# Attention and gated convolution on one core: a wider pitch for V, one product per second part, and a key copy on another engine

## The chip, the core and the metric

The kernel runs on one core of a Trainium2 chip. The core has five engines that follow programs of their own and meet at semaphores: TensorE (PE, matmuls, with its weight loads shown apart as PEld), VectorE (DVE), ScalarE (ACT), GpSimd (POOL), and SyncE (SP), which here only issues DMAs. Each engine works through its instructions in the order in which the program issued them. The metric is the device time of one execution in microseconds (us), lower is better. Before the change it is 219.84 us, the median of three runs that range from 218.36 to 220.60 us.

## The reference, cut to what matters

There are 8 batches with 8 heads each, 576 positions and a head size of 64. The mask works in blocks of 64 positions: a query sees all keys of its own block and of the blocks before it.

```python
scores = scale * np.matmul(q, k.transpose(0, 1, 3, 2))
scores = np.where(block_i >= block_j, scores, -1e9)
attn = softmax(scores)                       # over the keys
x = np.matmul(attn, v)                       # then heads side by side: 512 columns
gate_pre[s] = sum over k of conv_w[k] * x[s - 4 + k]      # causal convolution, 5 taps
out = (sigmoid(gate_pre) * (x @ w_val)) @ w_out
```

## The kernel before, in words

Two heads make a pair; there are 32 pairs, four to a batch, and the main loop (L536) takes two of them, a and z = a + 1, in each of 16 turns. Everything is unrolled, and the order on every engine is the order in which the lines run: the program is written under a manual schedule, with no planner that moves instructions. Tiles are guarded region by region: an instruction waits for the last writer of the elements that it reads.

For one pair the work is this.

- **Loads and casts.** SP loads K, Q and V as 32-bit floats (`load_qk`, L99, and `load_v`, L112). `cast_qk` (L126) and `cast_v` (L130) turn them into 16-bit floats, on POOL but for the first casts. V goes into the tile `ve` as rows of 64 elements, each followed by a one (the ones are written once, at L463), so that a product with V also gives the sum of the exponentials. The last 64 keys of V are loaded by batch and stand in `vtail`.
- **Transposes.** `trans` (L137) has PE transpose K or Q into PSUM, and DVE copies the result into `kT` or `qT` (L151). `kT` holds nine key blocks of 64. For K a second copy (L154) puts key blocks 6 and 8 once more into slots 9 and 11, with zeros standing in slot 10.
- **Scores and exponentials.** `scores` makes three chunks of a pair, 0, 1 and 2, of 512 columns for each head. Only chunk 1 reads slots 9 to 11. The chunks alternate between two PSUM buffers (`S`). `exps` has ACT take the exponential of a chunk into `pt` (L189). After chunk 1 POOL copies a part into `pd` (L192) and clears a masked part (L196); after chunk 2 it clears another (L199). `burst` (L201) issues the scores of two chunks and then their exponentials.
- **Product with V.** `pv` (L205) has two parts. Part 0 makes query blocks 0 and 1 (six matmuls), part 1 query blocks 2 and 3 and the last 64 queries (24 matmuls). Each matmul has 128 columns of `pt` as weights and one row group of `ve` (65 columns) as the moving operand. DVE takes reciprocals of the sums (L231) and multiplies them in: four groups of 64 columns on 128 partitions (L233), and in part 1 two more groups on 64 partitions (L237). The result is `xn`, whose fifth column block belongs to the last 64 queries; its lower 64 partitions are cleared once at the start (L450).
- **Gated unit.** `xt_pair` transposes `xn` (PE, then DVE at L248), of whose columns only the first 576 are used. `gate` makes the convolution with diagonal weights on PE, a DVE step (L262) and a tanh on ACT (L265). `val` (PE, then DVE at L277) and `out_tile` (PE, then ACT at L292, then a store) are kept in a list, and `filler` spreads them between the other steps. All matmul outputs other than scores share four PSUM buffers.

Ahead of the loop POOL gets, in this order, the cast of Q of pair 1, of V of pair 0, of the batch's V tails, of K and Q of pair 2 and of V of pair 1 (L525 to L530); only then come the four calls of `trans` for pairs 0 and 1 (L531 to L534). In the loop each `trans` of K stands just behind a cast of V:

```python
burst([(a, 0), (a, 1)])          # L546
...
burst([(a, 2), (z, 0)])          # L561
...                              # POOL: casts of K and Q of pair z + 2
cast_v(a + 2)                    # L572
trans(a + 2, "k")                # L573
pv(a, 0)
...
burst([(z, 1), (z, 2)])          # L594
cast_v(z + 2)                    # L596
trans(z + 2, "k")                # L597
pv(a, 1)
```

The weights `w_val` and `w_out` are loaded by DMAs that POOL issues in the first turn (L584). A slow exact path behind a flag is not taken with this data.

Of the kernel before, what the change touches and what calls it, by code (L numbers as in the profile page):

```python
# [16 lines left out]
def kernel(  # L17
# [10 lines left out]
    nc = tc.nc  # L28
    fp32 = mybir.dt.float32
    fp16 = mybir.dt.float16  # L30
    AF = mybir.ActivationFunctionType
    ALU = mybir.AluOpType
# [9 lines left out]
    def mm(out, lhsT, rhs, start=True, stop=True):  # L42
        nc.tensor.matmul(out=out, lhsT=lhsT, rhs=rhs, start=start, stop=stop,  # L43
                         skip_group_check=True)
# [3 lines left out]
    def const(shape, dtype, name):  # L48
        return cpool.tile(shape, dtype, tag=name, name=name)
# [10 lines left out]
    NV = 6  # L60
    NPT = 4
    NX = 4
    ves = [const([128, 2, 4, 65], fp16, f"ve{i}") for i in range(NV)]

    pts = [const([128, 2 * 1536 + 64], fp16, f"pt{i}") for i in range(NPT)]
    NT = 6
# [7 lines left out]
    xns = [const([128, 5, 128], fp16, f"xn{i}") for i in range(NX)]  # L74
# [15 lines left out]
    def bank(name, dtype=fp32):  # L90
        return psM.tile([128, 512] if dtype == fp32 else [128, 1024], dtype,
                        tag="misc", name=name)
# [44 lines left out]
    def trans(p, name):  # L137
        src = c16.pop((name, p))
        ps = bank("ps_tr", fp16)
        for t in range(6):  # L140
            nc.tensor.transpose(out=ps[:, 96 * t:96 * t + 96], in_=src[:, t, :, :],  # L141
                                identity=ident16[0:96, 0:96])
        if name == "k":
            dst = kTs[p % NT][:, 0:9, :].rearrange("p n x -> p (n x)")
        else:
            dst = qTs[p % NT][:, :]
        src = ps[:, 0:SEQ]
        if p < WIDE:
            dst = dst.rearrange("p (s t) -> p s t", t=6)
            src = src.rearrange("p (t s) -> p s t", t=6)  # L150
        nc.vector.tensor_copy(out=dst, in_=src)  # L151
        if name == "k":
            K = kTs[p % NT]
            nc.vector.tensor_copy(out=K[:, 9:12:2, :], in_=K[:, 6:9:2, :])  # L154


    COL = {0: 0, 1: 512, 3: 896, 2: 1024}
# [26 lines left out]
    def heads(p):  # L184
        return pts[p % NPT][:, 0:3072].rearrange("p (e x) -> p e x", e=2)
# [19 lines left out]
    def pv(p, part):  # L205

        b, j = divmod(p, PPB)
        pt, ve = heads(p), ves[p % NV]
        o = bank("ps_o")
        for c in (0, 1) if part == 0 else (2, 3):  # L210
            for e in range(2):
                g = 2 * (c % 2) + e
                for t in range(c + 1):
                    a = COL[t] + 128 * (c - t)
                    mm(out=o[:, 65 * g:65 * g + 65], lhsT=pt[:, e, a:a + 128],
                       rhs=ve[:, e, t, :], start=(t == 0), stop=(t == c))
        if part == 1:

            flat = pts[p % NPT]
            for e in range(2):  # L220
                dst = o[:, 260 + 65 * e:325 + 65 * e]
                for t in range(4):
                    a = 1536 * e + TAIL + 64 * t
                    mm(out=dst, lhsT=flat[:, a:a + 128], rhs=ve[:, e, t, :], start=(t == 0),
                       stop=False)
                mm(out=dst, lhsT=pds[p % NPT][:, 64 * e:64 * e + 128],
                   rhs=vtails[b % 2][:, 2 * j + e, :], start=False, stop=True)
        n = 4 if part == 0 else 6
        og = o[:, 0:65 * n].rearrange("p (g x) -> p g x", x=65)
        ri = rinv[:, p, 4 * part:4 * part + n].rearrange("p (g x) -> p g x", x=1)  # L230
        nc.vector.reciprocal(out=ri, in_=og[:, :, 64:65])  # L231
        x = xns[p % NX]
        nc.vector.tensor_tensor(  # L233
            out=x[:, 2 * part:2 * part + 2, :].rearrange("p c (e d) -> p (c e) d", e=2),
            in0=og[:, 0:4, 0:64], in1=ri[:, 0:4, :].to_broadcast([128, 4, 64]), op=ALU.mult)
        if part == 1:
            nc.vector.tensor_tensor(  # L237
                out=x[0:64, 4, :].rearrange("p (e d) -> p e d", e=2), in0=og[0:64, 4:6, 0:64],
                in1=ri[0:64, 4:6, :].to_broadcast([64, 2, 64]), op=ALU.mult)


    def xt_pair(p):
# [203 lines left out]
    nc.scalar.activation(out=warm[:, :], in_=ones[:, :], func=AF.Exp, bias=0.0, scale=0.125)  # L446
    make_identity(nc, ident)
    nc.vector.tensor_copy(out=ident16[:, :], in_=ident[:, :])
    for t in xns:
        nc.vector.memset(t[:, 4, :], 0.0)  # L450
    for t in kTs:
        nc.vector.memset(t[:, 10, :], 0.0)
    for t in vtails:
# [75 lines left out]
    cast_qk(2, "q", pool)  # L529
    cast_v(1)  # L530
    trans(0, "k")  # L531
    trans(0, "q")
    trans(1, "k")
    trans(1, "q")  # L534

    for a in range(0, NP, 2):  # L536
# [13 lines left out]
        if a:  # L550
            pv(z - 2, 0)
            filler(0.6)
            pv(z - 2, 1)
            xt_pair(a - 2)
# [16 lines left out]
        if a + 2 < NP:  # L571
# [3 lines that stand above are left out]
        if a + 2 < NP:  # L575
            trans(a + 2, "q")
# [94 lines left out]
```

## Time and profile before

| | |
|---|---|
| median of three runs | 219.84 us (218.36 to 220.60) |
| the profiled execution | 219.1 us, of which its span is 217.3 us |
| PE busy | 194.7 us, 90% of the span, 2806 matmuls |
| DVE busy | 156.2 us, 72% |
| ACT busy | 138.2 us, 64% |
| POOL busy | 103.4 us, 48% |
| DVE copies at L154 | 32, 7.7 us in all |
| DVE products at L233 and L237 | 64 and 32, 27.2 and 8.7 us |
| POOL casts of V at L131 | 32, 19.8 us |
| PE matmuls with `ve` as moving operand | 896, 39.8 us |

The profile shows one execution. The span runs from the first to the last instruction, and the execution's own time is 1.8 us longer. A matmul's duration is the time it spends in the array, and matmuls overlap there: the time that one costs is the distance from its start to the next one's. So a PE that is shown as busy may still be held back by short waits. "Idle before" names the wait of an engine ahead of an instruction and what ended it.

### The profile page before, as it was taken

The page shows a single profiled execution, that of the slowest core. Times are in us where ns is not written, and L with a number is a line of the kernel's source. Part 1 is how long each engine was busy: PE and PEld are TensorE (multiplying, and loading weights), DVE is VectorE, ACT ScalarE, POOL GpSimd, SP SyncE. Part 2 cuts the span into 40 slices and gives each one's busy share as a digit, 9 for nine tenths or more (in the row PEclk, how much of TensorE's full clock was granted, in tenths as well). Part 3 has the DMA queues.
Part 4 walks back from the last instruction along what each step waited for, and adds up shares of the span by engine and source line. Part 5 has one row for each costly group of instructions (what it writes and reads, how often), then busy time and mean ns, then how long its engine had stood idle before and what let it go on. Part 6 is the DMA issues. An engine that isn't in the chain of part 4 may idle for free. (4 is left out here: it accounts for less than half of the span.)

```text
span 217.3 us, 7199 instructions
## 1 busy us (share of the span) xinstructions
PE 194.7 (90%) x2806; PEld 138.7 (64%) x2806; DVE 156.2 (72%) x464; ACT 138.2 (64%) x197; POOL 103.4 (48%) x215
## 2 busy tenths in 40 slices
PE   1668784999999999999999999999999999999980
PEld 0447463676677766877587666876777767775730
DVE  3638993798668864988589676886688748968930
ACT  3257367265977679668875886758866797494330
POOL 4377726428473654645564638275645555210000
PEclk9999997699999999999999999999999999999995
DMA  6999999998199986999589979997999832011242
GB/s 173 237 237 227 208 267 202 182 212 172 52 244 254 185 219 160 257 199 216 147 208 207 218 201 247 204 190 161 216 250 228 206 103 98 0 51 48 100 166 87
DMA packets 104465, 39.34 MB, mean 181 GB/s; under 512 B 95717, under 2 KB 99813, under 8 KB 104426
## 3 DMA queue, kind: packets, MB, share of 16 engines
q1 hardware_dynamic: 103370, 37.77, 78.1%
q0 software_dynamic: 1056, 1.05, 2.9%
q8 instruction: 24, 0.39, 0.9%
q14 instruction: 15, 0.12, 0.2%
HBM read 30.42 MB, written 9.44 MB: 183 GB/s over the span
## 5 line engine op out<-in xcount | busy, mean ns | idle before, releaser
L189 ACT ACTIVATE pt<-S 128x1024 f16<-128x1024 f32 x96 | 92.5, 1020 | 20.6 <-PE S L43 20.6
L265 ACT ACTIVATE th<-th 128x288 f32<-128x288 f32 x64 | 27.9, 443 | 39.4 <-DVE th L262 38.8
L43 PE MATMUL ps_o<-ve,pt 128*128 128x65 f16 x896 | 39.8, 195 | 2.4 <-POOL pt L196 2.2
L192 POOL COPY pd<-pt 64x128 f16<-64x128 f16 x32 | 9.3, 292 | 62.9 <-ACT pt L189 62.7
L43 PE MATMUL ps_val<-xt,w_val 128*128 128x288 f16 x256 | 39.1, 290 | 0.0
L43 PE MATMUL ps_gate<-xt,diag 128*128 128x288 f16 x256 | 38.2, 291 | 0.7 <-DVE xt L248 0.3
L43 PEld LDWEIGHTS <-pt 128*128 128x128 f16 x896 | 34.9, 99 | 4.9 <-POOL pt L196 2.6
L43 PE MATMUL ps_out<-w_out,gv 128*128 128x512 f16 x144 | 35.7, 379 | 0.0
L43 PE MATMUL S<-qT,kT 64*128 64x64 f16 (+3 forms) x640 | 32.3, 237 | 2.7 <-ACT pt L189 2.5
L43 PEld LDWEIGHTS <-kT 64*128 64x128 f16 x640 | 18.5, 96 | 22.1 <-issue 17.3
L262 DVE SCALAR_TENSOR_TENSOR th<-xt,convT,ps_gate 128x288 f32<-128x288 f16 x64 | 30.3, 505 | 1.2 <-PE ps_gate L43 0.7
L43 PEld LDWEIGHTS <-diag 128*128 128x128 f16 x256 | 24.2, 99 | 9.3 <-issue 1.1
L233 DVE TENSOR_TENSOR xn<-ps_o,rinv 128x256 f16<-128x256 f32 x64 | 27.2, 424 | 2.2
L277 DVE SCALAR_TENSOR_TENSOR gv<-th,ps_val 128x288 f16<-128x288 f32 x64 | 27.5, 446 | 1.7 <-ACT th L265 0.5
L128 POOL CAST cq<-qst 96x768 f16<-96x768 f32 x31 | 25.6, 825 | 5.0 <-DMA qst<-in_q_dram 5.0
L43 PEld LDWEIGHTS <-w_val 128*128 128x128 f16 x256 | 24.0, 99 | 5.8 <-issue 0.2
L151 DVE COPY kT<-ps_tr 128x576 f16<-128x576 f16 x32 | 16.9, 528 | 13.2 <-PE ps_tr L141 13.1
L292 ACT ACTIVATE ob<-ps_out 128x512 f32<-128x512 f32 x34 | 20.1, 592 | 9.6 <-PE ps_out L43 6.7
L128 POOL CAST ck<-kst 96x768 f16<-96x768 f32 x30 | 24.6, 821 | 2.5 <-DMA kst<-in_k_dram 0.6
L131 POOL CAST ve<-vst 128x512 f16<-128x512 f32 x32 | 19.8, 617 | 8.6 <-DMA vst<-in_v_dram 7.8
L231 DVE RECIPROCAL rinv<-ps_o 128x4 f32<-128x4 f32 x64 | 12.1, 189 | 15.7 <-PE ps_o L43 13.8
L248 DVE COPY xt<-ps_xt 128x576 f16<-128x576 f16 x32 | 14.3, 449 | 11.6 <-PE ps_xt L246 11.6
(49 smaller groups left out, 179.8 us busy)
## 6 DMA issues: line engine op xcount, KB each, us to landing
out_dram<-ob SPq DMA_DIRECT2D x36, 256.0 KB, 2.8
vst<-in_v_dram SPq DMA_DIRECT2D x64, 128.0 KB, 4.2
kst<-in_k_dram SPq DMA_DIRECT2D x48, 144.0 KB, 3.9
qst<-in_q_dram SPq DMA_DIRECT2D x48, 144.0 KB, 4.0
kst<-in_k_dram SPq DMA_DIRECT2D x8, 288.0 KB, 6.9
qst<-in_q_dram SPq DMA_DIRECT2D x8, 288.0 KB, 7.0
vt<-in_v_dram SPq DMA_DIRECT2D x8, 128.0 KB, 4.7
w_val<-in_moe_w_val_dram POOLq DMA_DIRECT2D x1, 512.0 KB, 10.0
```

The costliest lines, as they stand in the source:

```text
L43: nc.tensor.matmul(out=out, lhsT=lhsT, rhs=rhs, start=start, stop=stop, skip_group_check=True)
L128: how(out=t[:, :, :, :].rearrange("p t e d -> p e t d"), in_=raw.pop((name, p))[:, :, :, :])
L131: nc.gpsimd.tensor_copy(out=ves[p % NV][:, :, :, 0:64], in_=vs.pop(p)[:, :, :, :])
L151: nc.vector.tensor_copy(out=dst, in_=src)
L189: nc.scalar.activation(out=pt[:, :, 512 * c:512 * c + 512], in_=ps[:, :, :], func=AF.Exp, bias=0.0, scale=0.125)
L231: nc.vector.reciprocal(out=ri, in_=og[:, :, 64:65])
L233: nc.vector.tensor_tensor(out=x[:, 2 * part:2 * part + 2, :].rearrange("p c (e d) -> p (c e) d", e=2), in0=og[:, 0:4, 0:64], in1=ri[:, 0:4 ...
L248: nc.vector.tensor_copy(out=xts[b % 2][:, g, PAD:PAD + SEQ], in_=ps[:, 0:SEQ])
L262: nc.vector.scalar_tensor_tensor(out=th, in0=xts[b % 2][:, g, s0 + 4:s0 + 4 + HALF], scalar=convT[:, g, 4:5], in1=gp[:, 0:HALF], op0=ALU.m ...
L265: nc.scalar.activation(out=th, in_=th, func=AF.Tanh, bias=0.0, scale=0.5)
L277: nc.vector.scalar_tensor_tensor(out=gvs[u][:, g, SEQ * bi + s0:SEQ * bi + s0 + HALF], in0=ths[b][:, g, s0:s0 + HALF], scalar=1.0, in1=vp[ ...
L292: nc.scalar.activation(out=ob[:, :], in_=ps[:, :], func=AF.Copy, bias=0.0, scale=0.5)
```

## The change

Three things change. The tile `ve` gets a pitch of 128 elements in place of 65; the matmuls still read 65 of them. In `pv` one product covers all groups of a part: in part 1 six groups on 128 partitions, in place of four on 128 and two on 64, and the clearing of the fifth block of `xn` at the start goes. The lower 64 partitions of that block then hold values that nothing reads. And the copy of key blocks 6 and 8 into slots 9 and 11 is issued to POOL in place of DVE, at the same place in the program.

```diff
-    ves = [const([128, 2, 4, 65], fp16, f"ve{i}") for i in range(NV)]
+    ves = [const([128, 2, 4, 128], fp16, f"ve{i}") for i in range(NV)]
@@ trans
             K = kTs[p % NT]
-            nc.vector.tensor_copy(out=K[:, 9:12:2, :], in_=K[:, 6:9:2, :])
+            nc.gpsimd.tensor_copy(out=K[:, 9:12:2, :], in_=K[:, 6:9:2, :])
@@ pv
-                       rhs=ve[:, e, t, :], start=(t == 0), stop=(t == c))
+                       rhs=ve[:, e, t, 0:65], start=(t == 0), stop=(t == c))
...
-                    mm(out=dst, lhsT=flat[:, a:a + 128], rhs=ve[:, e, t, :], start=(t == 0),
+                    mm(out=dst, lhsT=flat[:, a:a + 128], rhs=ve[:, e, t, 0:65], start=(t == 0),
...
-        x = xns[p % NX]
+        x = xns[p % NX][:, 2 * part:2 * part + n // 2, :]
         nc.vector.tensor_tensor(
-            out=x[:, 2 * part:2 * part + 2, :].rearrange("p c (e d) -> p (c e) d", e=2),
-            in0=og[:, 0:4, 0:64], in1=ri[:, 0:4, :].to_broadcast([128, 4, 64]), op=ALU.mult)
-        if part == 1:
-            nc.vector.tensor_tensor(
-                out=x[0:64, 4, :].rearrange("p (e d) -> p e d", e=2), in0=og[0:64, 4:6, 0:64],
-                in1=ri[0:64, 4:6, :].to_broadcast([64, 2, 64]), op=ALU.mult)
+            out=x.rearrange("p c (e d) -> p (c e) d", e=2), in0=og[:, :, 0:64],
+            in1=ri.to_broadcast([128, n, 64]), op=ALU.mult)
@@ setup
-    for t in xns:
-        nc.vector.memset(t[:, 4, :], 0.0)
```

## The prediction

> **What bounds the kernel now.** I read the stretches first: the first column is the stretch in us, then its length, then the busy time of PE, PEld, DVE, ACT and POOL with instruction counts, then the clock that PE was granted and the DMA share.
>
> ```profile
> 30.00:34.00 4.00, 2.35 (x55) 1.86 (x55) 3.93 (x14) 2.88 (x5) 0.85 (x3) 1.00 1.18 246
> 34.00:36.00 2.00, 0.96 (x17) 0.44 (x11) 0.46 (x2) 2.00 (x3) 1.62 (x4) 0.85 1.33 209
> 36.00:38.00 2.00, 0.96 (x15) 0.96 (x16) 0.26 (x1) 0.47 (x1) 1.88 (x4) 0.50 1.08 184
> 38.00:42.00 4.00, 4.00 (x23) 2.58 (x20) 3.50 (x8) 0.46 (x2) 2.28 (x4) 0.50 0.84 163
> 42.00:44.00 2.00, 2.00 (x53) 1.59 (x52) 1.12 (x2) 1.61 (x3) 0.04 (x1) 0.94 1.08 225
> 50.00:180.00 130.00, 129.32 (x1959) 92.64 (x1958) 97.31 (x289) 96.57 (x139) 72.25 (x142) 1.00 0.89 199
> ```
>
> From about 38 us on PE is never idle (129.32 of 130 us), while DVE, ACT and POOL have a quarter or more free: there the kernel takes as long as its matmuls. Before 37 us it is a ramp in which the DMAs are saturated. The clock is at half speed from about 35.4 to 42.2 us (0.85 and 0.94 of the two 2 us slices around it).
>
> Second, POOL's instructions in order of time (start, duration, line; in brackets the idle time before and what ended it), since two of the three edits touch it:
>
> ```profile
> 9.32 0.61 POOL L131 CAST ve<-vst 128x512 f16<-128x512 f32 x1 [0.55 <-DMA vst<-in_v_dram]
> ...
> 13.62 0.62 POOL L131 CAST ve<-vst 128x512 f16<-128x512 f32 x1 [0.53 <-DMA vst<-in_v_dram]
> 14.30 0.29 POOL L192 COPY pd<-pt 64x128 f16<-64x128 f16 x1
> ...
> 34.32 0.61 POOL L131 CAST ve<-vst 128x512 f16<-128x512 f32 x1 [3.07 <-DMA vst<-in_v_dram]
> 35.00 0.61 POOL L134 CAST vtail<-vt 64x512 f16<-64x512 f32 x1
> 35.55 0.30 POOL L192 COPY pd<-pt 64x128 f16<-64x128 f16 x1
> 35.79 0.31 POOL L196 MEMSET pt<- 64x256 f16 x1
> 36.17 0.82 POOL L128 CAST ck<-kst 96x768 f16<-96x768 f32 x1
> ...
> 107.02 0.29 POOL L192 COPY pd<-pt 64x128 f16<-64x128 f16 x1 [1.97 <-ACT pt L189]
> 107.25 0.31 POOL L196 MEMSET pt<- 64x256 f16 x1
> ```
>
> The row at 34.32 is the fence of the ramp: POOL waits 3.07 us for V of pair 5, and behind it stand the casts that PE needs. Third, PE in the ramp:
>
> ```profile
> 9.43 1.09 PE L43 MATMUL S<-qT,kT 64*128 64x512 f16 x10
> ...
> 14.90 0.51 PE L43 MATMUL ps_o<-ve,pt 128*128 128x65 f16 x6 [1.63 <-POOL pt L196]
> ...
> 37.04 0.66 PE L141 MATMUL ps_tr<-ident,ck 96*128 96x96 f16 x6 [1.57 <-POOL ck L128]
> ```
>
> At 37.04 the transposes of pair 6 start, released by POOL's cast of 36.17; from there PE hardly stops.
>
> **V's pitch.** Bytes and counts stay; POOL's cast still writes rows of 64. It takes 0.613 us at pitch 65. The casts of Q write rows of 64 at pitch 128 and take 0.825 us for 768 elements; at POOL's slope of 0.83 ns an element (memsets of 64x256, 309 ns, and 128x520, 529 ns) that makes 0.61 us for 512. So: nothing there.
>
> On PE it may matter. I took the starts of single matmuls in 23 second parts after 45 us. A matmul with 65 columns is followed by the next after 29.2 ns at some places and 32.6 ns at others, the same places in every pair. Slow are all that read the row group directly behind the one just read: t = 1, 2, 3 after t - 1, and also the second head's t = 0 where it follows the first head's t = 3, its neighbour in `ve`. Where the same t = 0 follows t = 1 or 2 or a row of `vtail`, it is fast, nearly always. Neither the start of a sum nor its end separates them. With pitch 128 nothing is adjacent any more: 126 bytes lie between two reads, and where the old kernel leaves 130 (second head's t = 0 after t = 2) it takes 29.2. By position, 17 of 24 matmuls in part 1 and 2 of 6 in part 0 are slow: 17 x 3.4 + 2 x 4 = 66 ns a pair. For the 28 pairs in the PE-bound stretch: 1.85 us. The bounds: nothing, if the cause is another (no row has this pitch), and 32 x 66 ns = 2.1 us. A loss I exclude: `w_out`, read at a pitch of 1024 bytes, runs at 216 ns per 512 columns, the same rate as the 29.2 (447 columns more in 186.8 ns, 0.42 ns each). I take 1.85, the nearest row.
>
> The Trainium skill, TensorE: Matmul & The Clock Gate, section "Back-to-back issue gap", speaks against this edit: the gap is N/2.4 + 2.5 ns whatever the address, 29.6 ns for 65 columns. The trace has that gap only at the places named; by the rule alone the edit would bring 0, by the rows 1.85 us.
>
> **One product.** L233 takes 424 ns, L237 272. Per 128 columns that is 152 ns, so six groups take 576 ns in place of 696: 3.8 us of DVE busy time. Counted from start to start (L233 0.345 us, L237 0.195), the saving is about 0.045 us a pair, 1.4 us. The memsets that go (4 x 0.11 us at 1.8 us) lie in DVE's wait for the first K; they bring nothing.
>
> **The copy, on DVE's side.** 32 x 0.24 = 7.7 us of busy time go. The median is 0.196 us; one at 25.18 us took 0.64, until POOL's cast of 24.94 us had ended. Start to start it costs 0.11 us, or 3.5 us in all, and 0.56 at 25.18.
>
> In the PE-bound stretch DVE's relief counts only where PE waited for DVE: ten waits of PEld after 42 us, behind L233, L237 and L277, 3.2 us in all. Each comes nearer by one or two of these savings, 0.05 to 0.15 us: **-0.5 us**, between 0 and -1.
>
> **The copy, on POOL's side.** The trace has no such copy on POOL. Nearest is L192, half as many partitions: 0.29 us, 0.24 from start to start. The vtail cast of 64 partitions (0.614) and V's of 128 (0.613) show that partitions don't count. Bounds: 0.20, what DVE took, and 0.61, a cast of four times the elements. I take 0.29, 0.24 in the queue; 32 of them add 9.3 us of POOL busy time.
>
> *Steady state.* Behind the copy stand L192, L196 and L199. POOL waits for ACT ahead of L192, never under 1.4 us after 42 us, so 0.24 vanishes. The copy's own input (L151) is done 2 us before POOL gets there, and chunk 1 of that pair is issued over 2 us later. Nothing: without this cover each would cost 0.24.
>
> *The start.* Here it is different. The first copy stands in POOL's queue behind the cast of V of pair 1, which waits for its DMA until 13.62 us and ends at 14.24. On DVE it ran at 7.50. Chunk 1 of pair 0 reads slots 9 to 11, so PE, which ran it in the row at 9.43, stops inside it until about 14.6: some 4.2 us. Behind it: exponential (0,1) at 15.1 in place of about 11; L192 of pair 0 at 16.15 in place of 14.30; the casts of pair 3, V of pair 2, and the two weight DMAs on POOL's own queue 2 us later; the product of pair 1, at 20.09 now, at 22.15: **2.05 us late**.
>
> How much survives the fence at 34.32? SP's loads up to V of pair 5 wait for none of the delayed casts, and its DMAs are saturated, so I leave 34.32 as it is. From 20.5 to 34 us DVE runs without a gap. Of the 2.05 us it gives back 0.56 and some 0.3 by the other savings, and may lose 0.5 where a diagonal's build comes to lie under POOL's cast of 28.39. ACT's exponential (4,1) ended at 34.66 and would be 1.2 to 2.0 late, 35.9 to 36.7. L192 of pair 4 needs it, and needs POOL: 35.55 plus the copy of pair 5, 35.79. It starts then 0.4 to 1.1 us late, and so does the restart of PE at 37.04. I take **+0.8 us**.
>
> The skill's same page, Part 1, says the array drops to half clock after an idle window of about 3.4 us on a free-running grid; the row at 36.00 agrees (0.50 after a stretch with 2.35 of 4 us busy). Applied to the new stop at 10 us it would, as an estimate from that page, hold the slow clock for one window more, at a price of some 1.7 us; no number below contains it.
>
> **Sum.** -1.85 - 0.5 + 0.8 = -1.55 us. On the profiled execution's 219.1 (span 217.3 and 1.8 around it) that is 217.55; that execution lay 0.74 below the median of 219.84, so for the median I say **218.3 us**.
>
> **Rivals.**
> 1. *The start is not absorbed* (slower). For: PE, ACT and POOL all stop with pair 0's chunk 1. Against: the 3.07 us and, at 28.39, 2.61 us that POOL idles for V. It decides if the DMA behind 34.32 moves with the stop, or if the lag at ACT's (4,1) stays above some 3 us. The whole 4.2 then reaches the end: 219.84 - 2.35 + 4.2 = 221.7, half of the time above 222.0. Chance 0.18.
> 2. *The pitch does nothing*: PE's gap of 32.6 ns is the weight load's. For: weight loads follow in the same rhythm. Against: they too run at 29 where the reads aren't adjacent. 219.84 - 0.5 + 0.8 = 220.1. Chance 0.17.
> 3. *The clock's dip goes.* Work before the fence comes later while the restart hardly moves, so PE's thin stretch (32.6 to 37.0) shortens by about 1 us. PE worked from 37.04 to 42.2 at half speed: 2.6 us. 218.3 - 2.6 = 215.7. Against: about 4 us of thin work remain. Chance 0.15.
>
> The forecast has the rest, 0.5, and 217.2 to 219.4 for itself (the runs of before spread by 1.1 either way). From 215.8 to 222.0 all but about 2 in 10 is held. A measurement of this kernel tells 1% (2.2 us) from no change. Faster by over 1%, below 217.6: rival 3 and a fifth of the forecast, 0.26. Slower, above 222.0: half of rival 1 and a little of rival 2, 0.12. The rest 0.62.
>
> **What would show it.** PE idle before a score matmul from 10 to 14.6 us, ended by POOL's copy. The 18 matmuls of a second part that took 0.74 us take 0.69. L192 of every second pair, 60.78 and 177.12 us now, ten turns apart, come 1.3 to 1.7 us closer together. DVE's busy time falls to about 145 us, POOL's rises to 113. The transposes of pair 6 start at 37.4 to 38.2. I am wrong if the distance over those ten turns stays at 116.3 us, or if POOL's wait for V of pair 5 is gone.

## The result, and the profile after

The changed kernel takes **217.19 us** (median of six runs, 216.09 to 218.32); the kernel before, run beside it, 220.03 us (six runs, 218.36 to 221.10). The ratio is 0.9876, with a 95% interval from 0.983 to 0.9921: 2.8 us are gone. The forecast was 218.3 us, its range 215.8 to 222.0.

Where the time went is told by one profiled execution of each, 219.1 us before and 216.53 after. I cut the span at three places that are the same matmuls in both:

| stretch of the span | before | after | difference |
|---|---|---|---|
| start to the K transposes of pair 6 | 37.04 | 37.15 | +0.11 |
| from there to the K transposes of pair 10 | 25.32 | 23.95 | -1.37 |
| from there to the start of the last matmul of the output | 148.10 | 146.49 | -1.61 |
| to the end of the span | 6.86 | 7.18 | +0.32 |
| span | 217.32 | 214.76 | -2.56 |

The windows of the kernel after, in the columns of the first fence of the prediction (stretch, length, then PE, PEld, DVE, ACT, POOL busy, clock, DMA share, GB/s):

```profile
36.00:38.00 2.00, 1.14 (x18) 0.97 (x17) 0.53 (x2) 1.30 (x2) 1.88 (x4) 0.79 1.18 198
38.00:42.00 4.00, 4.00 (x43) 2.77 (x40) 3.53 (x8) 0.74 (x2) 2.63 (x5) 0.68 1.04 184
...
50.00:180.00 130.00, 129.49 (x1975) 93.13 (x1972) 93.86 (x247) 97.66 (x142) 78.75 (x166) 1.00 0.88 200
```

Two things are to be seen. In the long stretch PE is still never idle, and more matmuls fit into it (1975 for 1959). And the clock is 0.79 and then 0.68 up to 42 us, in place of 0.50: the half-clock stretch is 3.41 us long (37.16 to 40.58) where it was 6.83 (35.40 to 42.23), so 43 matmuls run from 38 to 42 us in place of 23.

POOL after, by time (start, duration, line; in brackets the idle time before and what ended it):

```profile
13.51 0.61 POOL L131 CAST ve<-vst 128x512 f16<-128x512 f32 x1 [0.77 <-DMA vst<-in_v_dram]
14.07 0.53 POOL L154 COPY kT<-kT 128x128 f16<-128x128 f16 x2
...
34.20 0.61 POOL L131 CAST ve<-vst 128x512 f16<-128x512 f32 x1 [1.80 <-DMA vst<-in_v_dram]
34.75 0.29 POOL L154 COPY kT<-kT 128x128 f16<-128x128 f16 x1
35.10 0.61 POOL L134 CAST vtail<-vt 64x512 f16<-64x512 f32 x1
35.66 0.29 POOL L192 COPY pd<-pt 64x128 f16<-64x128 f16 x1
```

PE after, in the ramp:

```profile
14.41 0.34 PE L43 MATMUL S<-qT,kT 64*128 64x64 f16 x6 [4.14 <-POOL kT L154]
...
21.96 0.91 PE L43 MATMUL ps_o<-ve,pt 128*128 128x65 f16 x24 [0.58 <-POOL pt L196]
...
37.15 0.66 PE L141 MATMUL ps_tr<-ident,ck 96*128 96x96 f16 x6 [0.86 <-POOL ck L128]
```

PE stops for 4.14 us at the start, released by the copy that now stands behind V's cast, and the product of pair 1 comes at 21.96 us in place of 20.09. At 37 us little of that is to be seen in these two executions: POOL waits for V of pair 5 until 34.20 (before: 34.32), and the transposes of pair 6 start 2.95 us later (before: 2.72). The 0.23 us more are one copy, the row at 34.75. But two executions can't tell how much of the stop is left here. In the seven profiled kernels that have all key copies on DVE, and so the ramp of before, the transposes of pair 6 start anywhere from 37.04 (before) to 38.40 us; in the three with the stop and the early load of `w_out` it is 37.15, 37.17 and 38.71. A price below some 1.4 us would be lost in that.

Two groups of the table by line, operation and shape (count, then busy us and mean ns):

```profile
L233 DVE TENSOR_TENSOR xn<-ps_o,rinv 128x384 f16<-128x384 f32 x32 | 17.8, 557 | 1.1
...
L154 POOL COPY kT<-kT 128x128 f16<-128x128 f16 x32 | 9.4, 294 | 0.0
```

One product of six groups takes 557 ns where the two took 424 and 272. The copy takes 294 ns on POOL, where it took 240 on DVE.

### The profile page after: what moved, and what is told of

The parts are those of the page before. It is cut to its first block, busy times and chain, and to the rows that moved or that the text cites. A ratio compares the mean times of both kernels' runs of the same rounds, so it can differ in the third digit from the quotient of the medians.

```text
span 214.8 us, 7187 instructions
## 1 busy us (share of the span) xinstructions
PE 191.5 (89%) x2806; PEld 137.2 (64%) x2806; DVE 147.9 (69%) x396; ACT 138.4 (64%) x197; POOL 110.8 (52%) x247
## 5 line engine op out<-in xcount | busy, mean ns | idle before, releaser
L43 PE MATMUL ps_o<-ve,pt 128*128 128x65 f16 x896 | 38.6, 195 | 0.6 <-POOL pt L196 0.6
L192 POOL COPY pd<-pt 64x128 f16<-64x128 f16 x32 | 9.3, 292 | 56.7 <-ACT pt L189 56.7
L43 PE MATMUL ps_val<-xt,w_val 128*128 128x288 f16 x256 | 38.6, 288 | 0.0
L43 PE MATMUL ps_gate<-xt,diag 128*128 128x288 f16 x256 | 37.7, 289 | 0.4 <-DVE xt L244 0.3
L43 PE MATMUL S<-qT,kT 64*128 64x64 f16 (+3 forms) x640 | 32.5, 237 | 6.2 <-POOL kT L154 4.1
L43 PE MATMUL ps_out<-w_out,gv 128*128 128x512 f16 x144 | 35.6, 379 | 0.0
L43 PEld LDWEIGHTS <-pt 128*128 128x128 f16 x896 | 33.8, 98 | 2.7 <-POOL pt L196 0.7
L43 PEld LDWEIGHTS <-kT 64*128 64x128 f16 x640 | 18.2, 96 | 25.8 <-issue 16.2
L233 DVE TENSOR_TENSOR xn<-ps_o,rinv 128x256 f16<-128x256 f32 x64 | 31.4, 491 | 2.2
L43 PEld LDWEIGHTS <-diag 128*128 128x128 f16 x256 | 24.2, 98 | 8.5 <-issue 0.8
L43 PEld LDWEIGHTS <-w_val 128*128 128x128 f16 x256 | 23.9, 98 | 5.5
L151 DVE COPY kT<-ps_tr 128x576 f16<-128x576 f16 x32 | 16.8, 526 | 12.9 <-PE ps_tr L141 11.7
```

What stands on the lines that cost most here:

```text
L233: nc.vector.tensor_tensor(out=x.rearrange("p c (e d) -> p (c e) d", e=2), in0=og[:, :, 0:64], in1=ri.to_broadcast([128, n, 64]), op=ALU.mult)
```

## The experiments

The stretches named here are those of the table above: "the steady stretch" runs from the K transposes of pair 10 to the start of the last matmul of the output (before 148.10 us, after 146.49), "the four pairs" from pair 6 to pair 10 (25.32 and 23.95). Each is from one profiled execution. The steady stretch repeats within 0.1 us wherever the code in it is the same; the four pairs depend on the clock too. The runs of before that stood beside the experiments have medians between 219.4 and 220.4 us.

### Each part alone

**The pitch alone.** The copy is on DVE and there are two products, as before; only the tile changes:

```diff
-    ves = [const([128, 2, 4, 65], fp16, f"ve{i}") for i in range(NV)]
+    ves = [const([128, 2, 4, 128], fp16, f"ve{i}") for i in range(NV)]
```

> The kernel before with V at a pitch of 128 and nothing else changed. Theory (adjacent reads cost PE 3.4 ns a matmul): the 18 matmuls of a second part take 0.69 to 0.70 us in place of 0.74, the ten turns between two second-pair rows of L192 shrink by about 1.2 us, and the time falls by 1.8 us, ratio 0.992. If the clock's half-speed stretch stays as long as before, no more than that. Rival (the gain came from DVE's relief): ratio 1.000 and 0.74 us.

Measured: 219.25 us, ratio 0.9973 (0.9933 to 1.0013). The trace tells more than the median: the steady stretch is 147.36 us, **0.74 shorter**, and the 24 matmuls of a second part take 0.731 us in place of 0.764. So the pitch does something, and half of what was forecast.

**The copy on POOL alone.**

```diff
-            nc.vector.tensor_copy(out=K[:, 9:12:2, :], in_=K[:, 6:9:2, :])
+            nc.gpsimd.tensor_copy(out=K[:, 9:12:2, :], in_=K[:, 6:9:2, :])
```

> The kernel before with only the key copy on POOL. Theory (the stop at the start is taken up by the wait for V of pair 5 at 34.3 us): PE stands still from about 10.3 to 14.4 us, the restart at 37.0 moves by the 0.24 us of one copy, the steady part gains up to 0.4 us, and the half-speed stretch may be one window (3.4 us) shorter, as in the changed kernel, which is worth 0.9 us: ratio 0.994 to 1.001. Rival (the stop is paid): ratio 1.010 to 1.019.

Measured: 219.95 us, ratio 0.9994 (0.9962 to 1.0026). The steady stretch is 147.39 us, **0.71 shorter**, as much as by the pitch. In the profiled execution V of pair 5 came late (cast at 35.76, transposes of pair 6 at 38.71) and the half clock lasted 6.83 us, which hides the gain in its time; the mean clock of all ten runs, 0.976 to 0.982, is below the 0.983 to 0.985 of the changed kernel's six.

**One product alone.** The diff is that of `pv` and of the clearing of `xn`.

> The kernel before with only the one product in the second part. Theory: DVE isn't the bound; 0.045 us a pair of its time, off PE's path but for a few short waits: ratio 0.998 to 1.000. Rival (DVE's relief is what counts): ratio 0.994 or less.

Measured: 219.42 us, ratio 0.9949 (0.9903 to 0.9994). The steady stretch is 147.97 us, **0.13 shorter**, hardly more than the 0.1 by which it repeats. The interval would allow more, but the trace of the steady stretch doesn't show it; ahead of it single executions differ by more than that (see below), so the medians can't place it.

The three parts add up: 0.74 + 0.71 + 0.13 = 1.58 us, and the whole change has 1.61.

Why is the copy worth so much? DVE's instructions around it, before and then after (the same place in the program, near 109 us):

```profile
109.17 0.45 DVE L151 COPY kT<-ps_tr 128x576 f16<-128x576 f16 x1
109.65 0.25 DVE L154 COPY kT<-kT 128x128 f16<-128x128 f16 x1
109.76 0.17 DVE L231 RECIPROCAL rinv<-ps_o 128x4 f32<-128x4 f32 x1
```

```profile
107.60 0.45 DVE L151 COPY kT<-ps_tr 128x576 f16<-128x576 f16 x1
107.97 0.17 DVE L231 RECIPROCAL rinv<-ps_o 128x4 f32<-128x4 f32 x1
```

From L151 to the reciprocal it is 0.59 us with the copy and 0.37 without: the copy cost 0.22 us there. Its own start to the next start is 0.11, which is what I had put down. But the copy reads what L151 has just written, and starts 0.48 us behind it, where another instruction starts 0.37 behind it. That wait belongs to its price. It is so in 12 of the 24 pairs after 45 us, where the reciprocal's own input is ready. In the other 12 the reciprocal waits for PE in any case: it starts 0.76 us behind L151 with the copy and 0.69 with the copy moved, so there the copy cost 0.07.

The weight loads' waits for DVE after 42 us (total us, times, longest), in the kernel before:

```profile
PEld L43 <- DVE xn L233: 1.7, 5, 0.4
PEld L246 <- DVE gv L277: 0.7, 3, 0.2
PEld L246 <- DVE xn L233: 0.5, 1, 0.5
PEld L43 <- DVE xn L237: 0.3, 1, 0.3
```

and in the changed kernel:

```profile
PEld L242 <- DVE gv L273: 0.7, 3, 0.2
PEld L242 <- DVE xn L233: 0.7, 1, 0.7
PEld L43 <- DVE xn L233: 0.6, 3, 0.2
```

Together 2.0 us in place of 3.2. With the copy alone it is 1.6, with the pitch alone 3.2, with one product alone 3.3. So the relief is the copy's; of the 1.6 us of weight loads' waits that it takes away, 0.71 show in the stretch.

### The stop at the start

**The first two copies stay on DVE**, all else as in the changed kernel:

```diff
-            nc.gpsimd.tensor_copy(out=K[:, 9:12:2, :], in_=K[:, 6:9:2, :])
+            (nc.vector if p < 2 else nc.gpsimd).tensor_copy(out=K[:, 9:12:2, :], in_=K[:, 6:9:2, :])
```

> The changed kernel with the key copies of pairs 0 and 1 put back on DVE, so that the stop at the start goes; the other 30 copies stay on POOL. Theory (the ramp's fence takes the stop up): the product of pair 1 comes some 2 us earlier, the restart at 37.2 stays within 0.1 us, and the time is that of the changed kernel or slower by up to 0.9 us, if the half-speed stretch is again two windows long: ratio to the kernel before 0.987 to 0.992. Rival (the stop costs what it lasts): ratio 0.968 to 0.978.

Measured: 217.73 us, ratio 0.9887 (0.985 to 0.9924), the same as with the stop. The product of pair 1 comes at 20.71 us, so the stop is gone, and nothing is won. POOL and PE of this kernel, a little further on:

```profile
31.52 0.61 POOL L131 CAST ve<-vst 128x512 f16<-128x512 f32 x1 [5.00 <-DMA vst<-in_v_dram]
```

```profile
32.43 0.26 PE L43 MATMUL S<-qT,kT 64*128 64x64 f16 x6 [1.13 <-POOL kT L154]
```

POOL, which got there earlier, waits 5.00 us for V of pair 4. The copy of pair 4 stands behind that cast (at 32.08), so PE meets the same stop again, 1.13 us long, at a later pair. And V of pair 5 follows only at 35.38.

### Which reads are slow on PE

The gaps from each matmul's start to the next one's in one second part, in ns, as the trace has them (the parts that start at 59.52, 47.80, 48.37 and 69.74 us); the part has six sums, of 3, 3, 4, 4, 5 and 5 matmuls, the heads in turn:

```
pitch 65 (before)  29 35 33 29 32 33 29 32 33 32 33 32 33 32 30 33 32 33 29 29 35 33 32 29
pitch 66           29 35 33 29 32 33 29 33 32 33 29 32 33 32 29 33 32 33 29 29 34 32 33 29
pitch 72           29 35 29 30 29 29 35 29 29 29 30 35 29 29 29 29 35 29 30 29 29 35 29 29
pitch 128 (after)  29 35 29 29 29 35 30 29 29 29 35 29 29 30 29 35 29 29 29 29 35 30 29 29
```

At pitch 128 the gaps of 32 and 33 are gone, as forecast. What the prediction missed is a second pattern: about every sixth gap is 35. Five of 29 and one of 35 make 180 ns for six, 30 each; the mean of all is 30.4, not 29.2. Under the slow reads it hardly showed. Therefore 24 matmuls gain 33 ns and the six of the first part 4, **37 ns a pair and not 66**.

That it is the neighbourhood of the reads was tested in four ways, each kernel in a single timed run beside one of before, all with the copy on DVE and two products.

**Another order at pitch 65.** No read directly follows the row group before it:

```diff
-                for t in range(4):
+                for t in (1, 3, 0, 2):
```

and the orders (0), (1, 0), (0, 2, 1) and (1, 3, 0, 2) for the other sums, of one to four row groups.

> The kernel before, V's pitch of 65 kept, but the row groups of one sum taken in the order 1, 3, 0, 2 (0, 2, 1 where there are three, 1, 0 where there are two), so that no matmul reads the group directly behind the one just read. Adjacency theory: 24 matmuls of a second part take 0.73 us as with pitch 128, from 0.764. If an odd start address were the cause: 0.764 as before. If it were the accumulating itself: 0.764.

Measured: 218.36 us beside 220.15, 24 matmuls 0.735 us, steady stretch 147.43. The order alone does what the pitch does, without a byte more of memory. Where a read goes backwards to its neighbour (2, then 1) it is fast too.

**Pitch 66.** Two bytes lie between the reads, and each starts at a multiple of 4 bytes.

> The kernel before with V at a pitch of 66, two bytes between neighbouring reads, all starts on 4 bytes. If only touching or overlapping words count: 0.73 us for 24 matmuls. If reads that lie within the same few tens of bytes count: 0.76, as with pitch 65.

Measured: 219.30 us, 0.760 us, steady stretch 148.01: nearly as slow as before. One place differs: the second head's first row group, which follows its neighbour in the sum of four (the eleventh gap above), takes 29 or 30 ns in all 23 second parts after 45 us, and 32 or 33 at pitch 65, though 2 bytes are all that lies between there too.

**Pitch 97.** 64 bytes lie between the reads, and every other one starts off a multiple of 4.

> The kernel before with V at a pitch of 97: 64 bytes between neighbouring reads, every second start odd. Adjacency theory: 0.73 us for 24 matmuls. If it is the alignment of the start: 0.75 to 0.76.

Measured: 218.68 us, 0.732 us, steady stretch 147.41: as fast as pitch 128. So an odd start alone isn't slow; the end of the read before it matters.

**Pitch 72.** 14 bytes lie between the reads.

> The kernel before with V at a pitch of 72 elements in place of 65: 14 bytes lie between the end of one moving read and the start of the next. Pitch 66 (2 bytes) was slow, 0.760 us for the 24 matmuls of a second part, pitch 97 (64 bytes) fast, 0.732. If a read is slow only when it begins in the 16 bytes or fewer behind the previous one, 72 is still slow, 0.75 to 0.765; if a few bytes are enough, 0.73 to 0.74. Mixed, 0.74 to 0.75, if it hangs on where in a line of 32 or 64 bytes the reads end, since at this pitch of 144 bytes the rows end at other places in it each time. The time: 219.0 to 220.2, no verdict from one look.

Measured: 218.93 us beside 219.40, 0.732 us, steady stretch 147.44. Fourteen bytes are enough; two are not, but for the one place at pitch 66.

Distance alone doesn't explain that place; the offsets in `ve` do. If the tile begins at a multiple of 16 bytes, one rule fits the slow places at pitch 65 and 66 and their absence at 72, 97 and 128 and in the other order: a read is slow when its first byte lies in the same aligned 16 bytes as the last byte of the read before it. At pitch 66 the second head begins at byte 528, a multiple of 16, and the read before it ends with byte 525; all the other neighbours share their 16 bytes. At pitch 65 all do, at pitch 72 every read begins at a multiple of 16, and at 97 and 128 the reads lie too far apart. Blocks of 8 bytes would make the reads that begin at byte 264 of pitch 66 fast, and they are slow; blocks of 32 would make the one at 528 slow. The rule was worked out from these runs, and no run was made to test it; why it is so stays open.

### What holds the restart at 37 us

**The load of `w_out` two turns later.** The changed kernel, but the half megabyte that POOL loads in the first turn is issued in turn a = 4:

```diff
+        if a == 4:
+            load_w_out()
```

> The changed kernel with the 512 KB load of w_out issued two turns later (at about 41 us in place of 20), so that V of pairs 4 and 5 competes with 512 KB less. Theory (the wait for V of pair 5 is the fence, and with it gone the stop at the start is the bound): V of pair 5 arrives about 2 us earlier, POOL's wait for it shrinks to nothing, and the transposes of pair 6 come only 0.1 to 0.5 us earlier, held by ACT's exponential (4,1). Rival (the DMA alone sets the ramp): 2 us earlier, and the time falls by as much.

Measured: 217.16 us, ratio 0.9852 (0.9779 to 0.9926). POOL of this kernel:

```profile
32.76 0.61 POOL L131 CAST ve<-vst 128x512 f16<-128x512 f32 x1 [0.18 <-DMA vst<-in_v_dram]
...
35.71 0.29 POOL L192 COPY pd<-pt 64x128 f16<-64x128 f16 x1 [1.42 <-ACT pt L189]
```

V of pair 5 is there 1.4 us earlier, POOL's wait for it is nearly gone, and the transposes of pair 6 start at 37.20 us all the same. Now L192 of pair 4 waits 1.42 us for the exponential (4,1), which ends at 35.65 us (at 34.47 in the next kernel, which lacks the stop). The prediction had named this exponential as what would come next.

**The same, and the first two copies on DVE.**

> The same later load of w_out, and the key copies of pairs 0 and 1 on DVE: neither the stop at the start nor the fence. Theory: the transposes of pair 6 come 1 to 2 us earlier than with the stop, and the time is 1 to 2 us below that kernel's, 215.5 to 216.5 us: the stop's price where nothing takes it up. Rival (the stop is free in any case): both kernels within 0.5 us.

Measured: **215.37 us**, ratio 0.9765 (0.9707 to 0.9822). POOL:

```profile
32.68 0.61 POOL L131 CAST ve<-vst 128x512 f16<-128x512 f32 x1 [1.91 <-DMA vst<-in_v_dram]
...
34.53 0.29 POOL L192 COPY pd<-pt 64x128 f16<-64x128 f16 x1 [0.33 <-ACT pt L189]
```

The profiled execution, 216.95 us, is the longest of the four (the others 214.33 to 215.47); it has 10.2 us at half clock. But the transposes of pair 6 start at 36.02 us in it, 1.2 earlier, and the medians are 1.8 us apart. That points to a price of the stop, which lies under the wait for V in the changed kernel. It isn't shown: there are four runs of each, and the intervals overlap (0.9707 to 0.9822 here, 0.9779 to 0.9926 with the stop). What is shown is that without the stop the late load helps: 215.37 us here, 217.73 with the early load (0.985 to 0.9924). With the stop it brought nothing, and without the late load taking the stop away brought nothing. This version is faster than the kernel before, and its interval lies just below that of the changed kernel (0.983 to 0.9921).

### The clock

**Work for PE ahead of the fence.** The changed kernel with eight matmuls more, of 512 columns, whose output nothing reads; four stand behind each of the two `xt_pair` calls of turn a = 4:

```diff
+        if a == 4:
+            warm_mm(4)
```

> The changed kernel with eight matmuls of 512 columns that nothing reads, four behind each of the two transposes of xn in turn a = 4, where PE idles between 33.3 and 37.1 us. Theory: the half-clock stretch behind the fence (37.16 to 40.58 us in the changed kernel) is the echo of this thin stretch, and PE is the bound there, so without it L192 of turn 5 follows the transposes of pair 6 after 27.4 to 28.1 us in place of 29.11, and the time falls by 1.0 to 1.7 us from 217.2, to 215.5 to 216.2. Rival: behind the fence the casts on POOL and the exponentials hold PE as much as the clock does; then the clock shows full speed and the distance stays within 0.4 us of 29.1, the time at 217.2. If the eight matmuls delay the scores behind them, the transposes of pair 6 start later than 37.4 us.

The windows of this kernel, in the same columns as above:

```profile
36.00:38.00 2.00, 1.84 (x23) 1.04 (x23) 0.75 (x2) 1.35 (x2) 1.88 (x4) 1.00 0.90 180
38.00:42.00 4.00, 4.00 (x73) 3.22 (x74) 3.79 (x9) 1.50 (x3) 2.64 (x5) 1.00 0.82 180
```

The clock is at 1.00 throughout, and 73 matmuls run from 38 to 42 us where the changed kernel has 43. The transposes of pair 6 start at the same time (37.17 us), and the four pairs take 22.70 us in place of 23.95. So **a half-clock stretch of 3.41 us cost 1.25 us there**; the profiled execution is 1.30 us shorter than that of the changed kernel. The version with the late load agrees: without the extra matmuls, 6.12 us at half clock lie behind the start of the transposes, and the four pairs take 25.21 us; with them (the next kernel) 22.66. The medians show less: 216.59 us, ratio 0.9878 (0.9801 to 0.9955), which can't be told from the changed kernel's. The four runs spread from 215.23 to 217.79, with a mean clock of 0.992 to 0.994 in all of them, so their spread has another cause.

**The same in the version with the late load.**

> The same eight matmuls in the version with the late load of w_out and the first two copies on DVE (215.37 us). Theory: 1.0 to 1.7 us faster, 213.7 to 214.4 us, the half-clock stretch behind 36 us gone. Rival: no change, 215.4 us within 0.5, since there POOL and ACT, not PE, hold the work behind the fence.

Measured: 215.73 us, ratio 0.984 (0.9768 to 0.9913), no faster than without the extra matmuls; five runs from 213.12 to 216.89. In the profiled execution, the shortest, the clock is again at 1.00, the four pairs take 22.66 us, and the transposes of pair 6 start at 34.67, as V of pair 5 was cast at 31.53. So the trace shows the gain from the clock, and the median doesn't. With this spread the medians leave open what the extra matmuls are worth over many runs.

**When the clock falls.** Every change of the clock in a trace lies a whole number of 3.41 us from the others. If the span is cut into windows at these places, the kept traces separate by how much of a window PE is busy by the profile. In the ramp 13 windows at full clock are followed by one at half clock; PE is busy for 0.15 to 0.52 of them. The least busy window in the ramp that is followed by full clock has 0.525. A window at half clock is followed by another where PE is busy for 0.54, 0.79 or 0.83 of it, and by full clock from 0.87 on. So the two lengths of the stretch, 6.83 us before and 3.41 after, hang on where the windows lie: before, one begins at 35.40 us, 1.64 ahead of the restart, and is only 0.54 busy; after, one begins at 37.16, with the restart, and is full. Where the windows lie differs from execution to execution: the full clock is on record from 18.25 us in one and from 21.54 in another.

## Why the prediction was right, and where its terms were off

The number held, 218.3 forecast and 217.19 measured, but through terms that were off in both directions. Against the profiled executions the sum was -1.55 us and the span lost 2.6. That the errors of the pitch (too much), of DVE's relief and of the clock (too little) and of the ramp nearly cancel is luck.

1. **V's pitch, -1.85 forecast.** The mechanism was right: the slow gaps sat at adjacent reads, and they went. The size was wrong by nearly half: 37 ns a pair, 28 x 37 = 1.0 us in place of 1.85. The mis-sized term is "17 x 3.4 + 2 x 4 = 66 ns": it took the fast gap of 29.2 ns as what every matmul would get. Under the slow reads there was a second limit, one gap of 35 in about six, which hardly shows in the trace before. A rule by which a gap depends on the number of columns alone sees neither of the two. The Trainium skill, TensorE: Matmul & The Clock Gate, section "Back-to-back issue gap", gives such a rule for the isolated gap, from which 29.6 ns for 65 columns is an estimate; it says nothing of addresses. Here the same 65 columns took 32.6 or 29.2 ns by where the read before them ended, and 30.4 in the mean. The rival by which the pitch does nothing has fallen.

2. **DVE's relief, -0.5 forecast, between 0 and -1.** The waits were named rightly, and they fell from 3.2 to 2.0 us. In the steady stretch alone the copy brought 0.71 and the product 0.13 us; with some 0.5 in the four pairs ahead of it (below) that is 1.3, outside the range. Mis-sized is "start to start it costs 0.11 us": the copy held DVE for 0.22 where the next instruction was ready, since it also waited for the copy of L151 whose output it reads. The five waits at L43 for L233, 1.7 us in all, are two of 0.4 us with the copy alone. The product's saving was put at 0.045 us a pair and was worth next to nothing, as no long wait was behind it.

3. **The ramp, +0.8 forecast.** The stop came nearly as drawn: forecast until 14.6 us, measured until 14.41; L192 of pair 0 forecast at 16.15, measured 15.95; the product of pair 1 forecast 2.05 us late, measured 1.87. What survives is +0.11 in place of 0.8 in these two executions; kernels with the ramp of before differ by 1.4 us there, so its true size stays open. Exponential (4,1) was to be 1.2 to 2.0 us late; the first exponential of its burst starts at 33.55 in place of 32.72, 0.83 late, so L192 was not held by it (35.66 in place of 35.55, one copy more and V 0.12 earlier). In these executions the step that was mis-sized is the lag at ACT, not the fence: 34.32 taken "as it is" was 34.20. In the version with the late load, where the fence is gone, the lag at ACT does hold L192, by 1.42 us. The further window of slow clock that the prediction priced outside its sum isn't to be seen: the full clock is on record from 18.87 to 21.06 us in the four kernels with the stop, and from 18.25 to 21.54 in the ten without.

4. **Rival 1, the start not absorbed,** didn't come; POOL's wait for V, which the prediction gave against it, was still there with the stop (1.80 us). That the stop is hidden and not free is what the late load of `w_out` without and with it points to, 215.37 and 217.16 us, with intervals that overlap.

5. **Rival 3, the clock's dip goes,** came by half in the profiled execution. The stretch at half clock is 3.41 us in place of 6.83. What that is worth comes from kernels with the old copy on DVE whose profiled execution has the short stretch: with one product alone the four pairs take 24.75 us, with pitch 66 24.60, before 25.32; so 0.57 to 0.72 us of the 1.37 are the clock's. The rest, 0.65 to 0.8, is pitch and copy again. PE's thin stretch did shorten by about 1 us, as the rival had it (32.6 to 37.0 us before, 33.7 to 37.15 after), but that is not why: a whole window still fell into it (PE busy for 0.35 of it, 0.52 before), and the half clock is shorter since the next window began with the restart. The prediction's reading of an idle window fits only in part, too: PE was busy for half of the window that ended at 35.40. That the change caused the shorter stretch is not shown: single executions of before differ in their clock as well. The mean clock of the 47 runs of before beside the experiments lies between 0.967 and 0.992; the 24 with 0.985 or more have a median of 220.07 us, and the other 23 of 220.88. So even with the higher clock, which is above the changed kernel's 0.983 to 0.985, before stays 2.9 us above it: the 2.8 us between the medians don't hang on the clock.

6. **The end, not forecast.** From the start of the last matmul of the output to the end of the span it is 7.18 us in place of 6.86. Other kernels of this study have 6.9 to 7.5 there, with nothing changed in it.

The sum by what was measured: 0.11 - 1.37 - 1.61 + 0.32 = -2.55 us of span. By cause, the pitch is worth 0.9 to 1.0 us: 0.74 in the steady stretch, and 0.13 to 0.31 in the four pairs, which take 24.44 to 24.47 us at pitch 72 and 97 and in the other order, against the 24.60 and 24.75 above (four times 37 ns is 0.15). The kernel with pitch 128 alone can't be used here: its 24.23 us have 0.46 us of the half clock ahead of the four pairs. The copy and the product together are worth 1.3 us: 0.84, and 0.5 in the four pairs (23.95 after against 24.45).

The signs that were named: the score matmul stops until 14.41 us, ended by POOL's copy, as said. The 18 matmuls of a second part take 0.71 us, not 0.69. The two L192 ten turns apart are at 59.51 and 174.66 us, 115.15 in place of 116.34, so 1.2 closer and not 1.3 to 1.7. DVE's busy time is 147.9 us, not 145, since overlapping instructions are counted once: the second product had lain under its neighbours (one product alone lowers DVE's time by 0.9 us only), and so had part of the copy (6.5 us). POOL's is 110.8, not 113, for the same reason. The transposes of pair 6 come at 37.15, just ahead of "37.4 to 38.2". POOL still waits for V of pair 5, 1.80 us in place of 3.07.

## What to carry to other kernels

A slow pattern that is taken away uncovers the next limit, so the fastest gap seen in a trace is a bound of the gain and not its size. The price of an instruction in a full queue is how much closer its neighbours come without it, its wait for its own input included, not the distance from its start to the next one's. And where two delays lie over each other, as the stop at the start and the wait for V do here, removing one of them showed nothing; before either is called free, both have to be removed.

## What the runs showed of the hardware that was not expected

- A matmul whose moving operand begins 0 or 2 bytes behind the end of the one just read holds the next one back by about 3.4 ns (0.764 and 0.760 us for 24 matmuls at pitch 65 and 66), but not where it begins at a multiple of 16 bytes in `ve` (29 ns at byte 528 of pitch 66). From 14 bytes on it doesn't (0.732 and 0.731 us at pitch 72, 97 and 128), nor when the reads come in another order (0.735).
- Without that, a stream of matmuls of 65 columns with a weight load each does not run at an even 29 ns: about one gap in six is 35, and the mean is 30.4 ns. What sets it stays open.
- The same copy of 128x128 16-bit elements takes 294 ns on POOL and lengthens its queue by 0.23 us; on DVE it took 240 ns in the mean and lengthened the queue by 0.22 where the next instruction was ready.
- In the ramp the half clock came in stretches of 3.41 us or twice that, 6.83, between 35 and 45 us (once another one at 25), in every profiled execution but the two in which PE's thin stretch ahead of the fence had been filled. The Trainium skill, TensorE: Matmul & The Clock Gate, Part 1, has an idle window of about 3.4 us behind which the clock is halved; the length agrees, but PE needn't be idle: the windows ahead of these stretches had it busy for 0.15 to 0.52 of their time, and for 0.84 and 0.90 in the two kernels with extra matmuls.
- When V of a pair is there differs with what else is loaded, and from one execution to the next. Without the stop and with the early load, V of pair 4 was cast at 28.39, 29.07 and 29.14 us in three executions (before, other order, pitch 66) and between 31.14 and 32.07 in five. With the stop POOL issues the two loads of weights some 2 us later, and at 27.40, 27.47 and 28.34 us (after, extra matmuls, copy alone) the V was there before POOL was. That the later loads are the reason would fit, but the three early ones speak against it; it stays open, and so does what spreads the runs of one kernel by 2 us.
